# Cross-covariance attention and a GELU layer on one Trainium2 core: token blocks of 1024 in place of 512, other PSUM banks and a new order

## The chip, the core and the metric

The kernel runs on one core of a Trainium2 chip. Its engines run side by side, each with its own queue of instructions that it takes in order: TensorE (PE in the profile: matrix products, whose results go to PSUM), VectorE (DVE), ScalarE (ACT), GpSimd (POOL, used here mostly to issue DMAs), and SyncE (SP, issues DMAs). PSUM has 8 banks of 512 float32 per partition. The metric is the device time of one launch in microseconds.

## The reference

```python
qn = q / (norm(q, axis=1) + 1e-6)          # q, k, v: 4 x 6080 x 256, float32
kn = k / (norm(k, axis=1) + 1e-6)
a  = softmax(kn.T @ qn / tau, axis=-1)     # 256 x 256 per batch
x  = (v @ a).reshape(24320, 256)
h  = x @ w_in                              # 256 -> 2048
g  = 0.5*h*(1 + tanh(sqrt(2/pi)*(h + 0.044715*h**3)))
out = g @ w_out                            # 2048 -> 256
```

## The kernel before

**What it computes.** `v @ a @ w_in` is taken as `v @ (a @ w_in)`: per batch a matrix `AW` of 256 x 2048 is made from the scores, and then all 6080 tokens of the batch go through two products, `v . AW` (inner length 256, two halves `cc`) and `gelu(...) . w_out` (inner length 2048, in two halves `f` of 8 chunks of 128). All products take bfloat16.

**Scores of a batch.** q and k are loaded as bfloat16 in chunks of 6 rows per partition by `load_one` (L94, issued on the POOL queue; batch 0 has chunks of 8 and is loaded ahead of everything, L105 to L143). `square` (L181) squares a chunk on ScalarE or VectorE, `fold` and `fold_more` (L218, L226) add its rows on VectorE, `sum_parts` (L231) sums over partitions by a product. `gram_row` (L245) adds one row of `q.T k` to the running sum `G`, in bank `a`. A chain of small steps (L283 to L469) turns `G` and the norms into `AW`. For batches 1 to 3 this is spread between the token blocks of the batch before.

**Token blocks.** There are 12 blocks a batch, 48 in all, of 512 tokens (the last of a batch has 448). v goes to DRAM as bfloat16 by `cast_v` (L147, POOL queue) and comes back transposed by `load_vt` (L157, SP queue); the first three blocks are transposed on TensorE (L318). `mm1` and `gelu` (L511, L529) are the plain way: two chunks of 128 hidden columns in a pair of banks (`h` or `b`), four 512-column products, one gelu of 1024 values. The other way is a *set*: seven half-size products in place of eight (Winograd's form of Strassen's method; the halves are the tokens, the inner length, and two hidden chunk pairs `pa`, `pb`). `small` (L576) issues the products 1 to 7 of a set, each two of 256 columns, into a running sum `RB` (bank `s` or `p`) and the pair `QP` (`h` or `b`); `set_step` (L614) is what stands between them: `cq` and `y5` on ScalarE, `ap` and `ax` on VectorE, and the gelus `Gq`, `Gr`, `Gx`. A set costs ScalarE and VectorE more than the plain way and saves TensorE an eighth. `sums_w` and `sums_v` (L540, L552) make the operands. Blocks have two or three sets of four chunk pairs each (`sets_of`, L507).

The second product is taken by sevens too, on the block before: `sums_1` and `sums_2` (L693, L699) are differences of 2048 values a partition on VectorE, called T1 to T4; `product` (L716) issues M1 to M7, 8 products of 256 columns each, into the halves `r` and `p` of one bank `r`; `mm2_step` (L785) has its copies (`y5`, `cq` on ScalarE) and sums (`ap`, `ax` on VectorE); `turn` (L768) transposes a quarter of 256 values in VectorE, and `store` (L827) writes it out on the SP queue.

**The order.** Tile inserts the semaphores, but not the order: under `manual_schedule` each engine runs its instructions in the order in which the program calls them. The strings in `ORDER` (L998), one for each block, list all steps by short names: `g0` is a plain pair, `G0` its gelu, `w1m5` product 5 of set 1, `w1cq` its copy, `M5A` half of product M5, `row2` a Gram row, `lq`, `lk`, `lv`, `lt` the loads of q, k, v and the transposed v, `qsq` a square; a suffix counts blocks ahead or behind. A load of q, k or v carries a wait on the last product issued before it (`GATE`). So an instruction whose data are late holds up what stands behind it on its engine.

Of the kernel before, what the change touches and what calls it, by code (L numbers as in the profile page):

```python
# [17 lines left out]
def kernel(  # L19
# [14 lines left out]
    FC = D // 128  # L34
    assert isinstance(tau, (int, float)), "tau expected as a trace-time scalar"
    inv_tau = 1.0 / float(tau)

    R = N // 128
    REM = N - R * 128
    BLK = 512
    NB = (N + BLK - 1) // BLK
    PAIRS = FC // 2
    PE_BLOCKS = 2

    const = ctx.enter_context(tc.tile_pool(name="const", bufs=1))
    qkp = ctx.enter_context(tc.tile_pool(name="qkp", bufs=5))
    sqp = ctx.enter_context(tc.tile_pool(name="sqp", bufs=2))  # L50
    a1p = ctx.enter_context(tc.tile_pool(name="a1p", bufs=1))
    smx = ctx.enter_context(tc.tile_pool(name="smx", bufs=1))
    awp = ctx.enter_context(tc.tile_pool(name="awp", bufs=2))
    vts = ctx.enter_context(tc.tile_pool(name="vts", bufs=4))
    gp = ctx.enter_context(tc.tile_pool(name="gp", bufs=2))
    t1p = ctx.enter_context(tc.tile_pool(name="t1p", bufs=1))
    tsp = ctx.enter_context(tc.tile_pool(name="tsp", bufs=1))
    t4p = ctx.enter_context(tc.tile_pool(name="t4p", bufs=2))
    swp = ctx.enter_context(tc.tile_pool(name="swp", bufs=2))
    tvp = ctx.enter_context(tc.tile_pool(name="tvp", bufs=2))  # L60
    xp = ctx.enter_context(tc.tile_pool(name="xp", bufs=1))
    ywp = ctx.enter_context(tc.tile_pool(name="ywp", bufs=2))
    cp = ctx.enter_context(tc.tile_pool(name="cp", bufs=1))
    yout = ctx.enter_context(tc.tile_pool(name="yout", bufs=3))
    dram = ctx.enter_context(tc.tile_pool(name="dram", bufs=5, space=bass.MemoryType.DRAM))

    pM = ctx.enter_context(tc.tile_pool(name="pM", bufs=1, space=bass.MemoryType.PSUM))  # L70
    pH = ctx.enter_context(tc.tile_pool(name="pH", bufs=1, space=bass.MemoryType.PSUM))
# [16 lines left out]
    def after(inst, gate):  # L88

        if gate is not None:  # L90
            tc.add_manual_dep(inst.ins, gate.ins.name, mybir.DependencyInfo(
                mybir.DependencyClass.Sync, mybir.DependencyReason.DATA), reason="pace")

    def load_one(b, c, which, gate=None):  # L94
        r0, n = chunks_of(b)[c]
        t = qkp.tile([128, 8, 256], BF16, tag="qk"[which])
        src = (q, k)[which]
        after(nc.gpsimd.dma_start(  # L98
            out=t[:, 0:n, :],
            in_=src[b, 0 : R * 128, :].rearrange("(p r) c -> p r c", r=R)[:, r0 : r0 + n, :]), gate)  # L100
        if with_rest(b, c):
            after(nc.gpsimd.dma_start(out=t[:REM, n, :], in_=src[b, R * 128 : N, :]), gate)
        qk_tiles.setdefault((b, c), [None, None])[which] = t

    def load_first():  # L105


        r0, n = chunks_of(0)[0]
        assert not with_rest(0, 0)
        st = gp.tile([128, 2, n, 256], FP32, tag="g", name="qk_f32")  # L110
        for h in range(2):
            for which, eng in ((0, nc.sync), (1, nc.scalar)):
                eng.dma_start(out=st[:, which, h * 4 : h * 4 + 4], in_=(q, k)[which][0, 0 : R * 128, :].rearrange(
                    "(p r) c -> p r c", r=R)[:, r0 + h * 4 : r0 + h * 4 + 4, :])
        return st

    def cast_first(st):
        for which in range(2):
            t = qkp.tile([128, 8, 256], BF16, tag="qk"[which], name=f"first{which}")
# [7 lines left out]
    def load_qk(b, c):  # L127
        load_one(b, c, 0)
        load_one(b, c, 1)

    PIECES = [(0, 0, 4), (1, 0, 5), (1, 5, 8), (0, 4, 6), (0, 6, 8)]

    def load_last():
# [3 lines left out]
        qk_tiles[0, c] = [qkp.tile([128, 8, 256], BF16, tag="qk"[w], name=f"last{w}") for w in range(2)]  # L139
        for w, a, e in PIECES:  # L140
            nc.gpsimd.dma_start(
                out=qk_tiles[0, c][w][:, a:e, :],
                in_=(q, k)[w][0, 0 : R * 128, :].rearrange("(p r) c -> p r c", r=R)[:, r0 + a : r0 + e, :])  # L143

    v_bf = {}

    def cast_v(n, gate=None):  # L147
        b, blk = divmod(n, NB)
        t0 = blk * BLK
        cols = min(BLK, N - t0)  # L150
        vb = dram.tile([BLK, C], BF16, tag="vb", name=f"vb{n}")
        after(nc.gpsimd.dma_start(out=vb[:cols, :], in_=v[b, t0 : t0 + cols, :]), gate)
        v_bf[n] = vb

    vt_tiles = {}

    def load_vt(n):  # L157
        b, blk = divmod(n, NB)
        t0 = blk * BLK
        cols = min(BLK, N - t0)  # L160
        vT = vts.tile([128, 2, BLK], BF16, tag="vT")
        nc.sync.dma_start_transpose(out=vT[:, :, :cols], in_=v_bf.pop(n)[:cols, :])
        vt_tiles[n] = vT


    G, SS, SQ, SQR = {}, {}, {}, {}
# [8 lines left out]
    def new_squares(b, c):  # L175
        sq = sqp.tile([128, 8, 512], BF16, tag="sq", name=f"sq{b}_{c}")
        if with_rest(b, c):
            nc.vector.memset(sq[REM:, chunks_of(b)[c][1], :], 0.0)
        SQ[b, c] = sq

    def square(b, c, which, eng):  # L181
        if (b, c) not in SQ:
            new_squares(b, c)
        t = qk_tiles[b, c][which]
        n = chunks_of(b)[c][1]
        parts = [(128, slice(0, n))]
        if with_rest(b, c):
            parts.append((REM, slice(n, n + 1)))
        for np_, r in parts:
            o = SQ[b, c][:np_, r, which * 256 : which * 256 + 256]  # L190
            if eng == "act":
                nc.scalar.activation(o, t[:np_, r, :], AF.Square)  # L192
            else:
                nc.vector.tensor_mul(o, t[:np_, r, :], t[:np_, r, :])

    def square_rows(c, which, a, e, eng):
        if (0, c) not in SQ:
            new_squares(0, c)
        t = qk_tiles[0, c][which][:, a:e, :]
        o = SQ[0, c][:, a:e, which * 256 : which * 256 + 256]  # L200
# [5 lines left out]
    def fold_rows(b, c):  # L206

        n = len(rows_of(b, c))
        if n == 8:
            a1 = yout.tile([128, 4, 512], BF16, tag="ot", name=f"a1_{c}")  # L210
            nc.vector.tensor_add(a1, SQ[b, c][:, 0:4, :], SQ[b, c][:, 4:8, :])
            SQ[b, c] = a1
            n = 4
        SQR[b, c] = n

    FOLD = {}

    def fold(b, c):  # L218

        assert len(rows_of(b, c)) == 6  # L220
        sq = SQ.pop((b, c))
        a1 = a1p.tile([128, 3, 512], BF16, tag="a1", name=f"a1_{b}_{c}")
        nc.vector.tensor_add(a1, sq[:, 0:3, :], sq[:, 3:6, :])
        FOLD[b, c] = a1

    def fold_more(b, c, k):  # L226

        a1 = FOLD[b, c]
        nc.vector.tensor_add(a1[:, 0, :], a1[:, 0, :], a1[:, k - 1, :])

    def sum_parts(b, c):  # L231

        SS[b, c] = pM.tile([128, 4], FP32, tag="s", name=f"ss{b}_{c}")
        for j in range(4):
            nc.tensor.matmul(SS[b, c][:, j : j + 1], lhsT=FOLD[b, c][:, 0, j * 128 : j * 128 + 128],  # L235
                             rhs=ones_bf[:, 0:1], start=j == 0, stop=j == 3, skip_group_check=True)
# [8 lines left out]
    def gram_row(b, c, i):  # L245
        first = b not in G
        if first:
            G[b] = pM.tile([128, 2, 256], FP32, tag="a", name=f"G{b}")
        qt, kt = qk_tiles[b, c]
        rows = rows_of(b, c)  # L250
        r, np_ = rows[i]
# [8 lines left out]
    def ss_rows(c, which, rows=None):  # L260


        last = c == len(chunks_of(0)) - 1
        n = SQR.get((0, c), 8)
        rows = range(n) if rows is None else rows
        if c == 0:
            SS[which] = pM.tile([128, 2] if which == 0 else [128, 256], FP32,
                                tag="sp"[which], name=f"ss0{which}")
        sq = SQ[0, c]
        for r in rows:  # L270
            end = last and r == n - 1
            if which == 0:
                for jc in range(2):
                    nc.tensor.matmul(SS[0][:, jc : jc + 1],
                                     lhsT=sq[:, r, jc * 128 : jc * 128 + 128],
# [3 lines left out]
            else:  # L279
                nc.tensor.matmul(SS[1], lhsT=ones_bf, rhs=sq[:, r, 256:512],  # L280
                                 start=c == 0 and r == 0, stop=end)

    def g_copy(b):  # L283
        S = smx.tile([128, 2, 256], FP32, tag="S", name=f"S{b}")
        nc.scalar.activation(S, G[b], AF.Copy)
        G[b] = S

# [3 lines left out]

# [16 lines left out]
    V0 = []  # L308

    def load_v0(n):  # L310
        t = yout.tile([128, BLK // 128, C], BF16, tag="ot", name=f"v{n}")
        V0.append(t)
        nc.gpsimd.dma_start(out=t, in_=v[0, n * BLK : n * BLK + BLK, :].rearrange(
            "(s p) c -> p s c", p=128))

    VPS = {}

    def pe_vt(n, tag):  # L318

        VPS[n] = ps = pM.tile([128, 2, BLK], BF16, tag=tag, name=f"vt_ps{n}")  # L320
        for s in range(BLK // 128):
            for cc in range(2):
                nc.tensor.transpose(ps[:, cc, s * 128 : s * 128 + 128],
                                    V0[n][:, s, cc * 128 : cc * 128 + 128], ident_bf)

    def pe_vt_copy(n, cc):
        if n not in vt_tiles:
            vt_tiles[n] = vts.tile([128, 2, BLK], BF16, tag="vT", name=f"vT_pe{n}")
        nc.vector.tensor_copy(vt_tiles[n][:, cc, :], VPS[n][:, cc, :])

    def first_aw():

# [135 lines left out]

# [801 lines left out]
```

## Time and profile before

| | |
|---|---|
| median of 3 runs (lowest, highest) | 696.27 us (694.02, 703.08) |
| span of the profiled execution | 692.5 us |
| TensorE busy, matrix products | 671.3 us, 97%, 5643 records |
| VectorE busy | 630.7 us, 91%, 1111 |
| ScalarE busy | 624.0 us, 90%, 945 |
| DMA moved | 79.08 MB; mean busy share of the 16 DMA engines 0.9 and more in the first 100 us |
| granted TensorE clock | 0.999 |

The page gives the span of the profiled execution, from its first to its last instruction, and no time of the launch around it; the span lies 1.5 us under the fastest run and 3.8 us under the median. In the answers of the trace a row of a timeline is: start in us, duration in us, engine, line, operation, tiles, form, count, and in brackets the idle time before it with what ended it. The duration of a group of products reaches from the first start to the last end, and products overlap: the distance of starts is what the engine can sustain.

### The profile page before, as it was taken

To read this page: it belongs to the slowest core of one execution; us is meant where nothing else is said; L and a number is where in the kernel's file an instruction comes from. 1 tells how busy PE (TensorE), PEld (TensorE's weight loads), DVE (VectorE), ACT (ScalarE), POOL (GpSimd) and SP (SyncE) were. 2 spreads that over 40 slices of the span, in tenths; PEclk is the share of its full clock that TensorE was granted. 3 is DMA by queue.
4 is the path that set the end of the run, shared out by engine and by line. 5 is a ranking of instruction groups with operands and counts; after the bars stand their busy time and mean duration, and the time that the engine had idled before them with its cause. 6 is when DMAs were issued, how large, how long until landed. Compare 5 with 4: busy or idle time off the path is not lost.

```text
span 692.5 us, 14625 instructions
## 1 busy us (share of the span) xinstructions
PE 671.3 (97%) x5643; PEld 543.7 (79%) x5707; DVE 630.7 (91%) x1111; ACT 624.0 (90%) x945; POOL 74.4 (11%) x135
## 2 busy tenths in 40 slices
PE   3999999999999999999999999999999999999997
PEld 2856788888778888788877888878778888788886
DVE  3589999999999999999999999999999999899984
ACT  5379899999999899999999999999988999999984
POOL 4320111101001100110200011100100000000000
PEclk9999999999999999999999999999999999999999
DMA  9999799876766965686959495564263657142543
GB/s 242 207 269 130 138 153 132 119 126 107 129 117 111 164 94 92 100 144 110 140 83 156 85 162 89 98 103 85 33 107 60 104 93 100 39 77 47 94 71 59
DMA packets 161462, 79.08 MB, mean 114 GB/s; under 512 B 148448, under 2 KB 152160, under 8 KB 160672
## 3 DMA queue, kind: packets, MB, share of 16 engines
q0 software_dynamic: 14448, 39.72, 35.0%
q1 hardware_dynamic: 145696, 37.14, 32.4%
q10 hardware_dynamic: 1248, 1.28, 0.6%
q8 instruction: 44, 0.72, 0.5%
q14 instruction: 26, 0.21, 0.1%
HBM read 78.91 MB, written 36.57 MB: 167 GB/s over the span
## 4 chain that ended last, share of the span: by engine, by line
PE 88%; DMA 5%; issue 3%; ACT 2%; POOL 0%; DVE 0%; DVEq 0%; POOLq 0%
PE rp L736 39%; PE rb L604 15%; PE h L521 14%; PE qp L604 11%; PE G L253 5%; DMA t<-in_k_dram 4%; DMA t<-in_q_dram 1%; PE awp L454 1%; PE o L748 1%; ACT g L630 0%; ACT yw L623 0%; POOL t L98 0%; ACT qp L620 0%; ACT g L638 0%; PE ss L235 0%
## 5 line engine op out<-in xcount | busy, mean ns | idle before, releaser
L736 PEld LDWEIGHTS <-wcomb 128*128 128x128 bf16 x2632 | 255.4, 98 | 40.8 <-issue 1.6
L736 PE MATMUL rp<-t,wcomb 128*128 128x256 bf16 (+1 forms) x1504 | 208.1, 272 | 0.3
L736 PE MATMUL rp<-g,wcomb 128*128 128x256 bf16 (+1 forms) x1128 | 160.7, 272 | 0.1
L531 ACT ACTIVATE g<-h 128x1024 bf16<-128x1024 f32 (+1 forms) x136 | 137.5, 1017 | 12.5 <-PE h L521 10.9
L630 ACT ACTIVATE g<-qp 128x1024 bf16<-128x1024 f32 (+1 forms) x124 | 125.0, 1015 | 6.1 <-PE qp L604 3.9
L604 PEld LDWEIGHTS <-sw 128*128 128x128 bf16 x992 | 96.5, 98 | 22.9 <-issue 1.4
L521 PE MATMUL h<-vT,aw 128*128 128x512 bf16 (+1 forms) x406 | 111.8, 376 | 2.6
L625 DVE TENSOR_TENSOR qp<-rb,yw 128x512 f32<-128x512 f32 (+1 forms) x124 | 85.3, 689 | 9.4 <-PE rb L604 3.1
L604 PE MATMUL rb<-tv,sw 128*128 128x256 bf16 (+1 forms) x496 | 93.0, 271 | 0.1
L628 DVE TENSOR_TENSOR xw<-rb,yw 128x512 f32<-128x512 f32 (+1 forms) x124 | 83.7, 676 | 2.0 <-PE rb L604 1.0
L521 PEld LDWEIGHTS <-aw 128*128 128x128 bf16 x544 | 52.8, 98 | 38.9 <-DVE aw L362 0.6
L604 PEld LDWEIGHTS <-aw 128*128 128x128 bf16 x744 | 72.4, 98 | 12.9 <-issue 0.2
L638 ACT ACTIVATE g<-xw 128x512 bf16<-128x512 f32 (+1 forms) x124 | 77.3, 625 | 1.9 <-DVE xw L628 1.3
L620 ACT ACTIVATE qp<-rb 128x512 f32<-128x512 f32 (+1 forms) x124 | 72.3, 584 | 7.3 <-PE rb L604 3.2
L623 ACT ACTIVATE yw<-qp 128x512 f32<-128x512 f32 (+1 forms) x124 | 73.3, 596 | 3.0 <-PE qp L604 1.3
L635 ACT ACTIVATE g<-rb 128x512 bf16<-128x512 f32 (+1 forms) x124 | 72.5, 594 | 2.7 <-PE rb L604 2.2
L192 ACT ACTIVATE sq<-t 128x1536 bf16<-128x1536 bf16 (+4 forms) x49 | 64.5, 1336 | 6.1 <-DMA t<-in_q_dram 6.0
L774 DVE STREAM_TRANSPOSE ot<-rp 128x256 f32<-128x256 f32 (+1 forms) x141 | 59.8, 435 | 6.2 <-PE rp L736 4.8
L253 PE MATMUL G<-t 128*128 128x256 bf16 (+1 forms) x352 | 58.3, 276 | 1.3 <-DMA t<-in_k_dram 1.3
L711 DVE TENSOR_TENSOR t<-g,t 128x2048 bf16<-128x2048 bf16 (+1 forms) x47 | 56.7, 1206 | 0.7
L709 DVE TENSOR_TENSOR t<-g 128x2048 bf16<-128x2048 bf16 (+1 forms) x47 | 56.5, 1202 | 0.5 <-ACT g L638 0.4
L696 DVE TENSOR_TENSOR t<-g 128x2048 bf16<-128x2048 bf16 (+1 forms) x47 | 56.4, 1200 | 0.1
(131 smaller groups left out, 808.5 us busy)
## 6 DMA issues: line engine op xcount, KB each, us to landing
out_dram<-ot SPq DMA_DIRECT2D x174, 128.0 KB, 3.1
vb<-in_v_dram POOLq DMA_DIRECT2D x41, 256.0 KB, 4.9
t<-in_q_dram POOLq DMA_DIRECT2D x21, 384.0 KB, 5.7
t<-in_k_dram POOLq DMA_DIRECT2D x21, 384.0 KB, 4.9
wst<-in_moe_w_out_dram POOLq DMA_DIRECT2D x2, 1024.0 KB, 11.0
t<-in_q_dram POOLq DMA_DIRECT2D x3, 512.0 KB, 14.3
t<-in_k_dram POOLq DMA_DIRECT2D x3, 512.0 KB, 17.0
out_dram<-ot SPq DMA_DIRECT2D x12, 112.0 KB, 3.1
```

The lines of the kernel that those rows point to most:

```text
L253: nc.tensor.matmul(G[b][:, jc, :], lhsT=qt[:np_, r, jc * 128 : jc * 128 + 128], rhs=kt[:np_, r, :], start=first and jc == 0, stop=jc == 1, ...
L521: mm = nc.tensor.matmul(hp[:, u, :cols], lhsT=AW[b][:, cc, fc * 128 : fc * 128 + 128], rhs=vt_tiles[n][:, cc, :cols], start=cc == 0, stop= ...
L531: nc.scalar.activation(gs(n)[:, 2 * p : 2 * p + 2, :cols], HP.pop((n, p))[:, :, :cols], AF.Gelu_apprx_tanh)
L604: GATE[0] = nc.tensor.matmul(acc[:, u * hc : u * hc + hc], lhsT=lhs[:, u * 128 : u * 128 + 128], rhs=rhs, start=m in (1, 5) and u == 0, st ...
L620: nc.scalar.activation(qp(n, i)[:, 0, :c], RB[n, i][:, :c], AF.Copy)
L623: nc.scalar.activation(YW[n, i][:, :c], qp(n, i)[:, 1, :c], AF.Copy)
L625: nc.vector.tensor_add(qp(n, i)[:, 1, :c], RB[n, i][:, :c], YW[n, i][:, :c])
L628: nc.vector.tensor_add(XW[n, i][:, :c], RB[n, i][:, :c], YW.pop((n, i))[:, :c])
L630: nc.scalar.activation(gs(n)[:, 2 * pa : 2 * pa + 2, :c].rearrange("p u (t x) -> p t u x", t=2), QP.pop((n, i))[:, :, :c].rearrange("p t ( ...
L635: nc.scalar.activation(gs(n)[:, 2 * pb : 2 * pb + 2, :hc], two(RB.pop((n, i))[:, :c]), AF.Gelu_apprx_tanh)
L638: nc.scalar.activation(gs(n)[:, 2 * pb : 2 * pb + 2, hc:c], two(XW.pop((n, i))[:, :c]), AF.Gelu_apprx_tanh)
L736: nc.tensor.matmul(ACCS[n, acc][:, :hc], lhsT=wcomb[:, w, fc, :], rhs=x, start=first and k == 0, stop=k == 3, skip_group_check=True)
```

## The change

Every part of the kernel is written anew; the arithmetic is the same.

- **Blocks** are of 1024 tokens (the last of a batch 960; the last batch ends with 512 and 448): 25 blocks in place of 48. A plain step (`plain`) is one hidden chunk for 1024 tokens. Block 0 takes its tokens by halves (`half`, named `e` and `E`), all plain.
- **Sets** are of one chunk pair for 1024 tokens: a product of a set is one of 512 columns, not two of 256. A set is as much work as before. Six sets of eight in most blocks, three in block 1; over all there are 135 sets, of which 6 stand in the two small blocks, in place of 124.
- **Second product**: M1 to M7 have 512 columns. The sums `r` and `p` take a bank each, chosen in the order, in place of halves of one. T1 to T4 are as long as before, but T3 is written over a quarter of the gelu's result; there are two buffers each for T1/T4 and T2. `ap`, `ax`, `cq`, `y5` and the transposes work on 512 values, not 256.
- **Gram rows** come in three bursts a batch. A burst has its own running sum in whatever bank the order names; `gram_out` copies the first to SBUF on ScalarE and adds the next two there on VectorE.
- **Banks** `a`, `r`, `s`, `p` are named word by word in the order (`m1.1@r:1`), and no bank is kept for one purpose.
- **Buffers**: two of 1024 tokens for the transposed v, not four of 512; one for the v sums, not two; batch 0's q and k and `w_out` lie in the gelu buffers `g0b`, `g1a`, `g1b` ahead of their use, so that `w_out`'s first load waits for batch 0's last Gram row.
- **Order**: one string of words `step.args@bank:block`, new throughout. Ahead of it the loads are issued as before, but batch 0's v comes partly between those of `w_in`, and only tokens 0 to 1535 of v are transposed on TensorE, as before.

```diff
-    BLK = 512
+    for b in range(B):
+        sizes = [1024] * (N // 1024) + [N % 1024]
+        if b == B - 1:
+            sizes[-1:] = [512, N % 1024 - 512]
...
+    def gram_out(b):
+        g = G.pop(b)
+        if b not in GS:
+            GS[b] = smx.tile([128, 2, 256], FP32, tag="S", name=f"S{b}")
+            nc.scalar.activation(GS[b], g, AF.Copy)
+        else:
+            nc.vector.tensor_add(GS[b], g, GS[b])
...
-    def mm1(n, p):
+    def plain(n, u, tag):
+        b, _, t = BLOCKS[n]
+        hc = t // 2
+        hp = bank(tag, [128, 2, 512], f"h{n}_{u}")
...
+        for x in range(2):
+            BITS[tag, x] = w
+            for cc in range(2):
+                mm(hp[:, x, :w],
+                   lhsT=aw(b, cc, u if wide else 2 * u + x),
+                   rhs=vt_tiles[n][:, cc, x * hc : x * hc + hc] if wide else vt_tiles[n][:, cc, :],
+                   start=cc == 0, stop=cc == 1)
...
     def small(n, i, m, tag=None):
+        U = 1 if hc > 256 else 2
...
-        for u in range(2):
-            GATE[0] = nc.tensor.matmul(acc[:, u * hc : u * hc + hc], lhsT=lhs[:, u * 128 : u * 128 + 128],
-                             rhs=rhs, start=m in (1, 5) and u == 0, stop=u == 1,
-                             skip_group_check=True)
+        for u in range(U):
+            mm(acc[:, u * hc : u * hc + hc], lhsT=lhs(u), rhs=rhs,
+               start=m in (1, 5) and u == 0, stop=u == U - 1)
...
+    def token_sum(n, i, h):
+        if i == 3:
+            o = quarter(n, 0, 1, h)
+        else:
+            o = tp.tile([128, 4, 512], BF16, tag="tx" if i in (1, 4) else "ty", name=f"t{i}{h}_{n}")[:, :, :hc]
...
-    BANK = {1: "r", 2: "r", 3: "r", 5: "p", 6: "p", 7: "p", 4: "p"}
-                    rp = pM.tile([128, BLK], FP32, tag="r", name=f"rp{n}")
-                    ACCS[n, "r"], ACCS[n, "p"] = rp[:, 0 : BLK // 2], rp[:, BLK // 2 : BLK]
+        acc = "r" if i <= 3 else "p"
+        first = i in (1, 5) and (n, acc) not in ACC
+        if first:
+            ACC[n, acc] = bank(tag, [128, 512], f"{acc}{n}")
...
-    """g0 lv+3 aw3 G0 aw2 g1 ac2 ac3 aw4 G1 aw5 lq+1 ac4 g2 ac5 g3 G2 aw6 G3 g4 ac6 SW0 aw7 G4 g5
-    lk+1 ac7 vtp G5 pA11 g6 vtc0 g7 vtc1 G6 T1a vtq G7""",
+ORDER = """
+lq.0:1 e.1_0@h:0 lk.0:1 E.1_0:0 aw.2@s:0 aw.3@a:0 e.0_0@b:0 ac.2:0 vp.1@r:0 ac.3:0 e.3_0@h:0
+vc.1_1:0 vc.1_0:0 aw.5@p:0 aw.4@s:0 ac.5:0 lq.1:1 E.0_0:0 aw.6@a:0 E.3_0:0 qsq.0:1 e.2_0@b:0
+e.0_1@h:0 lv.1:1 E.2_0:0 E.0_1:0 aw.7@r:0 e.3_1@b:0 E.3_1:0 e.2_1@h:0 vp.0@p:1 e.1_1@b:0 E.2_1:0
+ac.4:0 ac.6:0 lk.1:1 SW.0:0 e.4_0@h:0 E.1_1:0 row.0_5@s:1 ksq.0:1 e.5_0@b:0 lv.0:2 pA11:0 E.4_0:0
...
```

## The prediction

> **What bounds the kernel now.** I read the page's totals first, then the busy time by stage, then single rows of the timelines.
>
> ```profile
> span 692.5 us, 14625 instructions
> ...
> PE 671.3 (97%) x5643; PEld 543.7 (79%) x5707; DVE 630.7 (91%) x1111; ACT 624.0 (90%) x945; POOL 74.4 (11%) x135
> ```
>
> ```profile
> 100.00:150.00 50.00, 49.74 (x434) 41.26 (x437) 47.27 (x83) 48.34 (x73) 6.91 (x13) 1.00 1.01 136
> 200.00:250.00 50.00, 49.74 (x432) 42.03 (x436) 47.70 (x90) 45.08 (x74) 5.25 (x11) 1.00 0.74 126
> 400.00:450.00 50.00, 49.82 (x436) 41.91 (x438) 46.73 (x81) 49.25 (x73) 5.69 (x11) 1.00 0.68 116
> ```
>
> The columns of the second are the stretch, its length, and the busy time of TensorE, its weight loads, VectorE and ScalarE. From 40 to 680 us TensorE is idle for some 4 us in all; it is the bound. But ScalarE and VectorE stand at 90 to 98% of the same stretches: there is little room under it. The first 37 us are another stage: batch 0's loads keep the DMA engines full and TensorE waits for data.
>
> Whether TensorE is busy says nothing of its pace. That is read from runs of equal products:
>
> ```profile
> start us, us, engine line op out<-in xcount [idle before <-releaser]
> 6.85 1.89 PE L253 MATMUL G<-first,first 128*128 128x256 bf16 x8 [6.85 <-ACT first L122]
> 28.60 1.91 PE L253 MATMUL G<-t 128*128 128x256 bf16 x16 [0.60 <-DMA t<-in_k_dram]
> 41.11 1.89 PE L521 MATMUL h<-vT_pe,aw 128*128 128x512 bf16 x8
> ```
>
> One product of 256 columns lasts 0.27 us, so 15 starts of the second row take 1.64 us: 109.4 ns each. Eight of 512 columns (41.11 to the next row at 42.84) take 1.73: 216.2 ns. The two fit 2.6 ns a product and 0.417 ns a column. The first row, after an idle start, has half that pace: 7 starts in 1.47 us, 210 ns for 256 columns.
>
> **The change part by part.**
>
> *Products.* From the two programs I count 5,704 products of 1,551,408 columns before and 3,576 of 1,545,648 after. The fewer columns are eleven more sets (135 for 124), each with an eighth less. 2,128 x 2.6 ns = 5.5 us, 5,760 x 0.417 ns = 2.4: **-7.9 us**, all on the path while TensorE is the bound. Width alone is nearly worthless, since time goes by columns. The Trainium skill (TensorE: Matmul & The Clock Gate, "Back-to-back issue gap") gives 131 ns as the sustained distance of 512-column products in a real stream and 216 ns as that of isolated ones; the trace's 216.2, taken in a stream with weight loads, is the second.
>
> *ScalarE and VectorE.* Eleven more sets cost ScalarE 0.588 + 0.600 + 0.598 + 0.630 + 1.024 us for two gelus of 1.025 each: +15 us of row means. Copies of the second product are half as many and twice as long, 0.59 for 2 x 0.37: -7.5. Squares moved to VectorE: -3. In sum ScalarE +4. VectorE: +15 for `ap`, `ax` of the added sets; v sums of 1024 values in fewer instructions -11; second product's sums (0.69 for 2 x 0.43) -7; transposes of 512 values, which the trace does not show: 0.44 at least, as for 256, 0.87 at most, as for two; I take 0.66, since the add grows by 1.6 from 256 to 512. That is -16 for 92 of them, with 20 either way. The six new adds of Gram sums are 0.69 each, as `ap`: +4. With the rest VectorE -7. None of this is on the path by itself.
>
> *Where they stand in the order.* I cut both orders into twelve stretches of 53.5 us of products and sum each engine's row means there (less 0.07 us an instruction on ScalarE, 0.055 on VectorE: their means add up to 693 us each, busy is 624 and 631, as neighbours overlap). Before, the worst stretch has 53.5 us of TensorE, 55.6 ScalarE, 56.6 VectorE; the trace shows no idle TensorE there, so about 3 us is carried by buffers. After, the fourth has 54.0, **59.3**, 55.9, and the seventh 53.6, 57.3, 56.6; the excess of all stretches is 11 us for 4 before. What passes 3 us of carry is 3.6 here and 2.7 to 6.5 with other cuts. I take **+5 us**; the bounds are 0 and the whole excess with shorter cuts, 15 above before's.
>
> *The first load of batch 1.* This is a wait that the change adds. The 21st word of the new order, `qsq.0:1`, puts the square of q's first chunk of batch 1 on ScalarE, ahead of the gelu `E.2_0`. In the old order the chunk is used 13 us of products after its load is issued. Here it is 5. When does it land? The rows of before:
>
> ```profile
> 36.23 0.90 POOL L655 DMA_DIRECT2D wst<-in_moe_w_out_dram  x1 [0.21 <-PE vt_ps L323]
> 38.98 0.54 POOL L152 DMA_DIRECT2D vb<-in_v_dram  x1 [1.86 <-PE h L521]
> 40.72 0.57 POOL L98 DMA_DIRECT2D t<-in_q_dram  x1 [1.19 <-PE h L521]
> ```
>
> ```profile
> wst<-in_moe_w_out_dram POOLq DMA_DIRECT2D x1, 1024.0 KB, 12.4
> t<-in_q_dram POOLq DMA_DIRECT2D x1, 384.0 KB, 10.8
> ```
>
> The second fence is the DMA view of those two issues, the last number being us from issue to landing. `w_out`'s second half lands at 48.6 us, v's cast at 49.7, q at 51.5, the k after it at 53.3: loads of the POOL queue land one by one in the order of issue, 1.8 us for 384 KB. After the change the same bytes stand ahead of that q but for v's cast. Issued at 37 instead of 41, it lands at **50.4**: earlier issue does not help, the bytes ahead do. ScalarE is at `qsq.0:1` at 42.6. TensorE's products up to `e.3_1` sum to 7.4 us from 37.65, so it reaches it at 45.0 and needs bank `b` there, which `E.2_0` frees: 50.4 + 1.4 (the square) + 1.0 = 52.8. **+7.8 us**. (VectorE waits likewise for k, until 52.2, with the copy `ac.7` behind it; TensorE wants that copy 8 us of products later: nothing more.) Below: if q were to land 4.9 us after issue, the median later on, nothing.
>
> *The pace after it.* The first bursts of the trace (idle to 6.85, then from 8.74 to 11.67) run at half pace until about 18.4, some 3.5 us of unbroken products. No row has a long idle time behind the full pace; the nearest is this start. So the loss is between nothing and half of 3.5 us; I take **+1.7**. The profile's granted clock, 1.00 there, does not show it. The Trainium skill (TensorE: Matmul & The Clock Gate, "Part 1: The HAM clock gate") has it as a rule, 1.2 GHz after an idle window of 3.4 us and 2.4 after a busy one; by it the loss is an estimated 1.7 us too. The trace agrees in so far as the two bursts, of 1.9 us each, did not bring the full pace and 3.5 unbroken us did.
>
> *Other waits.* Transposed v has two buffers, not four: counting from the store ahead of it on SP and the cast, the shortest leads of its 45 loads are 6.3, 6.9 and 9.7 us for 10.8 before, landing is 2.8 to 12.8, median 4.5. Loads of q and k have leads of 5.4, 5.6, 5.9 us where 8.1 was the shortest; they land in 4.2 to 11.9, median 4.9. The last block's stores have block 23's last quarter behind them, one more transpose and issue. Together **+1.5**, at most 6. Between a bank's last product and the next owner's first there are at least 0.43 us of products, as before (0.44), also with sums in banks of their own: nothing. `w_out`'s first load waits for batch 0's last Gram row (34.2 us, before it left at 33.6), behind a queue full until 40: nothing. The first 37 us are DMA's in both.
>
> *The sum*: -7.9 + 7.8 + 1.7 + 5 + 1.5 = +8.1. The span goes from 692.5 to 700.6. The span lies 3.8 us under the median of the runs, 696.27; with the same around it the time is **704 us**, 1.2% slower, which 2%, about what a measurement of this kernel can tell, calls no change.
>
> **The rivals.**
>
> *No wait and an order that fits* (0.24). Loads land in time, buffers carry the stretches: -7.9 + 2 gives 690. For it: before hides 3 us in a stretch. Against: loads landed in order without exception.
>
> *ScalarE and VectorE become the bound* (0.27). If the carry ends where a stretch is over by more than about 1 us, in place of 3, the excess of shorter cuts counts, 15 us for 5, and a longer transpose adds to it: 714 to 720, slower by over 2%. For it: after 37 us ScalarE and VectorE each need 96% of TensorE's time by these sums, for 94 and 96 before. Against: before shows next to none of it.
>
> *Wide products overlap in a long stream* (0.02), so that time no longer goes by columns and TensorE is not the bound. ScalarE is then: 624 + 4 us of work, and before's idle 21 up to 40 us and 8 after 680: 657, with 3.8 around it 661. The row with 216.2 ns speaks against it. The Trainium skill's 131 ns, named above, is this rival's rule.
>
> **How the numbers follow.** Forecast 0.47, its own range 698 to 710 by the stretches' and the other waits' ends. The range 690 to 718 leaves out the third rival, about half of the first (under 690), and the far end of the second. Faster by over 2% (under 682) 0.03: -7.9 alone ends at 688. Slower by over 2% (over 710): 0.27. Within: 0.70.
>
> **What would show it.** Right: groups of 512-column products at 216 ns; ScalarE's waits led by `sq` for `in_q_dram`, 7 to 8 us, ahead of the fourth gelu; TensorE idle from 45 to about 53 and the products after it at 430 ns for 512 columns; idle TensorE at 200 to 255 us, where the fourth stretch lies. Wrong: that q landing before 45; TensorE with under 6 us of idle time after 60; ScalarE's sum over 645.

## The result, and the profile after

The changed kernel takes **764.89 us** (median of 4 runs, 764.42 to 765.68) beside 695.16 us for the kernel before (694.02 to 703.08): a ratio of 1.098, 95% interval 1.092 to 1.104. It is 10% slower. The forecast was 704 with a range of 690 to 718, so it was wrong in size and in verdict.

The page's totals:

```profile
span 763.2 us, 10047 instructions
...
PE 687.0 (90%) x3518; PEld 336.5 (44%) x3579; DVE 629.6 (82%) x931; ACT 628.3 (82%) x935; POOL 74.4 (10%) x137
```

The work of VectorE and ScalarE is what it was (630.7 and 624.0 before), in a span that is 70.7 us longer. No engine is full. Busy time by stage (stretch, length, TensorE, weight loads, VectorE, ScalarE, POOL, granted clock, DMA share, GB/s):

```profile
40.00:60.00 20.00, 12.82 (x61) 6.08 (x60) 10.38 (x18) 9.34 (x10) 1.61 (x3) 0.83 0.83 205
100.00:150.00 50.00, 47.20 (x244) 22.96 (x248) 44.49 (x66) 46.22 (x67) 6.35 (x11) 1.00 0.67 105
200.00:250.00 50.00, 47.02 (x215) 20.83 (x218) 45.80 (x70) 42.95 (x67) 4.68 (x9) 1.00 0.60 99
400.00:450.00 50.00, 46.02 (x220) 20.59 (x223) 45.99 (x70) 45.87 (x68) 5.24 (x10) 1.00 0.79 129
```

One loss is early, as forecast. The other runs through the whole kernel: TensorE, which stood at 49.7 to 49.8 of 50 us, is at 46 to 47, and the two others fall with it. The waits (engine, tile and line, what it waited for: us in total, times, longest) say between whom:

```profile
PE qp L482 <- DVE qp L605: 13.9, 20, 1.2
...
PE rb L482 <- ACT qp L600: 8.0, 17, 0.7
PE e L482 <- ACT g L525: 7.0, 1, 7.0
PE qp L482 <- ACT yw L603: 5.6, 12, 1.3
...
ACT qp L600 <- PE qp L482: 32.2, 52, 1.7
...
DVE qp L605 <- ACT yw L603: 25.8, 33, 2.3
DVE qp L605 <- PE qp L482: 20.8, 22, 2.8
```

Of these rows all but the wait of `e` are steps of the sets, and most concern `qp`, the pair of banks that a set works in. Before, `cq` lost almost nothing to products that write the pair:

```profile
ACT qp L620 <- PE qp L604: 1.6, 3, 0.8
```

The chain of work that ended last shows the same, first for the changed kernel, then for the kernel before:

```profile
PE 63%; ACT 19%; DVE 9%; issue 3%; DMA 3%; POOL 0%; DVEq 0%; POOLq 0%; SPq 0%; ACTq 0%
```

```profile
PE 88%; DMA 5%; issue 3%; ACT 2%; POOL 0%; DVE 0%; DVEq 0%; POOLq 0%
```

What such a wait is can be seen in one set (timeline: start, duration, what, and the idle time before it with its releaser):

```profile
318.00 0.38 PE L482 MATMUL qp<-tv,sw 128*128 128x512 bf16 x1
...
318.41 0.58 ACT L600 ACTIVATE qp<-rb 128x512 f32<-128x512 f32 x1 [1.24 <-PE qp L482]
...
319.05 0.38 PE L482 MATMUL rb<-tv,sw 128*128 128x512 bf16 x1 [0.67 <-ACT qp L600]
...
319.38 0.60 ACT L603 ACTIVATE yw<-qp 128x512 f32<-128x512 f32 x1
...
320.04 0.38 PE L482 MATMUL qp<-vT,aw 128*128 128x512 bf16 x1 [0.62 <-ACT yw L603]
...
320.25 1.89 PE L482 MATMUL r<-g,wcomb 128*128 128x512 bf16 x8
...
320.45 0.70 DVE L605 TENSOR_TENSOR qp<-rb,yw 128x512 f32<-128x512 f32 x1 [1.51 <-PE qp L482]
```

These are product 5, `cq`, product 6, `y5`, product 2 and `ap` (and, at 320.25, eight products of the second product). Product 5 writes the second bank of the pair. `cq` copies `rb` into the *first* bank and reads nothing that product 5 makes; product 1, which it copies, had ended at 316.2. ScalarE stood idle for 1.24 us ahead of it, and it began 30 ns after product 5 ended. Product 2 adds to the first bank and waits for `y5`, which reads the second. `ap` writes the second bank and waits for product 2, which writes the first. These three waits have no datum behind them. The pair is one tile of 128 x 2 x 512, and the program's waits in PSUM are drawn by whole tile: the second bank is taken for the first. The wait of product 6 for `cq` is a true one (it adds to the bank that `cq` reads), and passes the delay on.

This was so before the change, too; the new order makes these pairs of steps neighbours more often. Counted in the two programs, before to after: `cq` waits for a product 5 issued behind product 1, from which `cq` has its data, in 40 of 124 sets, then in 89 of 135; product 2 stands ahead of `ap` in none, then in 45; after the change, product 2 waits for `y5` of its own set in 25.

**Where the 70.7 us are.** TensorE goes on to its next product 2.6 ns + 0.417 ns a column after the last one began, when nothing holds it (the forecast's term). What the distances of starts exceed that by is time without starts (times from the first counted instruction, 0.24 us into the span; products that the trace lacks are made up for):

| us | 0 to 40 | 40 to 60 | after 60 | start of the last product |
|---|---|---|---|---|
| before | 11.1 | 0.1 | 7.7 | 687.3 |
| after | 11.6 | 9.8 | 73.6 | 755.3 |

Without them the products take 668.4 and 660.3: **-8.1**. (This figure uses the forecast's own pace, so it does not test it. The row at 320.25 does: eight products of 512 columns in 1.89 us, as at 41.11 us before.) To that come +0.5 and +9.7 in the first two columns, **+65.9** in the third, and 2.7 more behind the last product's start: 70.7.

### The profile page after: what moved, and what is told of

It is laid out like the page before. It is cut to its first block, busy times and chain, and to the rows that moved or that the text cites. A ratio compares the mean times of both kernels' runs of the same rounds, so it can differ in the third digit from the quotient of the medians.

```text
span 763.2 us, 10047 instructions
## 1 busy us (share of the span) xinstructions
PE 687.0 (90%) x3518; PEld 336.5 (44%) x3579; DVE 629.6 (82%) x931; ACT 628.3 (82%) x935; POOL 74.4 (10%) x137
## 4 chain that ended last, share of the span: by engine, by line
PE 63%; ACT 19%; DVE 9%; issue 3%; DMA 3%; POOL 0%; DVEq 0%; POOLq 0%; SPq 0%; ACTq 0%
PE p L482 15%; PE rb L482 11%; PE r L482 11%; PE qp L482 9%; PE h L482 9%; ACT qp L600 5%; PE G L205 4%; ACT yw L603 4%; DVE qp L605 3%; ACT g L624 3%; ACT g L613 2%; ACT g L505 2%; ACT sq L158 2%; DVE t L691 2%; DMA q<-in_q_dram 2%
## 5 line engine op out<-in xcount | busy, mean ns | idle before, releaser
L482 PEld LDWEIGHTS <-wcomb 128*128 128x128 bf16 x1408 | 136.3, 97 | 166.9 <-issue 27.9
L482 PE MATMUL p<-t,wcomb 128*128 128x512 bf16 (+2 forms) x564 | 142.1, 372 | 1.3 <-ACT g L624 0.4
L605 DVE TENSOR_TENSOR qp<-rb,yw 128x512 f32<-128x512 f32 (+2 forms) x135 | 92.9, 689 | 60.1 <-ACT yw L603 25.8
L482 PE MATMUL r<-g,wcomb 128*128 128x512 bf16 (+2 forms) x564 | 140.8, 372 | 1.6 <-ACT p L751 0.9
L600 ACT ACTIVATE qp<-rb 128x512 f32<-128x512 f32 (+2 forms) x135 | 78.3, 583 | 42.6 <-PE qp L482 32.2
L691 DVE TENSOR_TENSOR t<-g,t 128x2048 bf16<-128x2048 bf16 (+2 forms) x96 | 113.0, 1183 | 0.1
L482 PE MATMUL rb<-tv,sw 128*128 128x512 bf16 (+3 forms) x281 | 98.7, 367 | 12.4 <-ACT qp L600 8.0
L505 ACT ACTIVATE g<-h 128x1024 bf16<-128x1024 f32 (+1 forms) x94 | 95.4, 1024 | 13.2 <-PE h L482 12.7
L608 DVE TENSOR_TENSOR xw<-rb,yw 128x512 f32<-128x512 f32 (+2 forms) x135 | 91.4, 678 | 15.3 <-PE rb L482 10.2
L482 PE MATMUL h<-vT,aw 128*128 128x512 bf16 (+2 forms) x383 | 98.6, 376 | 1.3 <-ACT g L613 0.2
L603 ACT ACTIVATE yw<-qp 128x512 f32<-128x512 f32 (+2 forms) x135 | 79.9, 595 | 8.4 <-PE qp L482 6.5
L482 PE MATMUL qp<-tv,sw 128*128 128x512 bf16 (+3 forms) x141 | 49.8, 367 | 4.1 <-ACT g L505 2.6
```

What stands on the lines that cost most here:

```text
L482: GATE[0] = nc.tensor.matmul(*a, skip_group_check=True, **kw)
L505: nc.scalar.activation(g_half(n, u // 8)[:, u % 8].rearrange("p (t x) -> p t x", t=2), hp[:, :, :hc], AF.Gelu_apprx_tanh)
L600: nc.scalar.activation(QP[n, i][:, 0, :w], RB[n, i][:, :w], AF.Copy)
L603: nc.scalar.activation(YW[n, i][:, :w], QP[n, i][:, 1, :w], AF.Copy)
L605: nc.vector.tensor_add(QP[n, i][:, 1, :w], RB[n, i][:, :w], YW[n, i][:, :w])
L608: nc.vector.tensor_add(XW[n, i][:, :w], RB[n, i][:, :w], YW.pop((n, i))[:, :w])
```

## The experiments

The texts on record name the explanations by letters. P is the waits between a pair's two banks. L is the load of the engines, ScalarE and VectorE having too much to do beside TensorE (the forecast's second rival). T is an order that leaves too little time between steps that truly depend on each other. B, in the text of the first reordered kernel, is the shared banks or the two buffers of v. The texts also work with a replay of the order, which is an estimate: each engine takes its instructions in the program's order, with durations from the trace and the traced delays between engines. It gives 689 us for before and 755 for after, where the spans are 692.5 and 763.2. It knows nothing of how loads share the DMA engines.

### The two banks as two tiles

```diff
-            QP[n, i] = bank(tag, [128, 2, 512], f"qp{n}_{i}")
+            QP[n, i] = pair(tag, f"qp{n}_{i}")
...
-            nc.scalar.activation(QP[n, i][:, 0, :w], RB[n, i][:, :w], AF.Copy)
+            nc.scalar.activation(QP[n, i][0][:, :w], RB[n, i][:, :w], AF.Copy)
...
-                nc.scalar.activation(g[:, k0].rearrange("p (t x) -> p t x", t=2), qp[:, :, :hc],
+                ge = nc.scalar.activation(g[:, k0].rearrange("p (t x) -> p t x", t=2), twice(qp[0], hc),
```

Every pair, those of the plain steps too, is two tiles of one bank. A gelu can read only one tile, so it reads the first bank twice. What this kernel leaves out is the gelu of the second banks; the number of values and the waits are the same. The order is the changed kernel's.

> The changed kernel in its own order, but the two banks of a pair (tags h and b) are two tiles, so that a step on one bank no longer waits for a step on the other. A gelu over a pair reads its first bank twice (as many values in the same form, so ScalarE's work is the same), and waits for the last products of both banks; what is left out is the gelu of the second banks. Theory P (pair): in the changed kernel 'cq' waits for m5 in 89 of 135 sets, m2 for 'ap' in 38, 'ap' for m2 in 26 and 'y5' for 'cq' in 94, and these waits, not the load, hold the engines. An estimate: each engine takes its instructions in this order, with the durations and hops of the trace (37 ns from a product's end to ScalarE or VectorE, 51 to 53 ns back); that gives 755 us for the changed kernel's span of 763, and 692 without the waits inside pairs. So P expects a span of 692 to 705, with under 20 us of idle TensorE after 60 us, for 74. Theory L (load; the rival B of the prediction): ScalarE and VectorE do as much work in the same order, so the span stays at 750 to 763. Theory T (the order leaves too little time between steps that truly depend on each other): most of the loss stays, over 740.

Measured: **702.51 us** in one execution, span 700.7. The page, the busy time of a stretch, and of TensorE's waits the longest and the longest for a step of a set:

```profile
PE 672.5 (96%) x3579; PEld 335.0 (48%) x3579; DVE 624.3 (89%) x931; ACT 616.8 (88%) x935; POOL 73.8 (11%) x137
```

```profile
400.00:450.00 50.00, 50.00 (x273) 24.90 (x271) 48.71 (x73) 49.21 (x75) 5.50 (x11) 1.00 0.73 125
```

```profile
PE e L491 <- ACT g L536: 7.1, 1, 7.1
...
PE qp L491 <- ACT qp L618: 0.4, 1, 0.4
```

TensorE is full again from 400 to 450 us; its waits for the steps of a set, 13.9, 8.0 and 5.6 us above, are down to 0.4 at most. Time without starts after 60 us falls from 73.6 to 11.3. So **62 us** of the loss are waits between two banks of one pair. L falls with it: ScalarE and VectorE do nearly the same work here (616.8 and 624.3 us for 628.3 and 629.6) and the span is 62.5 us shorter. So does T, which expected over 740: the steps that truly depend on each other stand as they did. Late loads after 60 us are out as well, since the loads are the same.

### Two of the waits put back

In the kernel with the banks apart, `cq` is made to wait for product 5 again; in another, product 2 and `ap` wait for each other again, in the changed order's direction. The gelu of the second banks is left out in both.

```diff
+            cq = nc.scalar.activation(QP[n, i][0][:, :w], RB[n, i][:, :w], AF.Copy)
+            after(cq, M5[n, i])
```

```diff
+            if m == 2 and u == 0:
+                after(GATE[0], AP.get((n, i)))
...
+            after(AP[n, i], M2.get((n, i)))
```

> As e1_halves_apart (702.5 us; it leaves out the gelu of the second banks), and one of the waits put back by hand: each 'cq' waits for m5 of its set, which writes the other bank of the pair. Theory P with this wait as the main part: by the order with the trace's durations 692 becomes 725, so 702 becomes 730 to 738, and ScalarE's waits are led by 'cq' for m5. If the waits matter only together (theory P, all at once): under 715.

> As e1_halves_apart (702.5 us; the gelu of the second banks is left out), and the other wait put back: of m2 and 'ap' of a set, which write the two banks of the pair, the one that is issued later waits for the one issued earlier (45 sets have m2 first, 90 'ap'). By the order with the trace's durations 692 becomes 716, so 702 becomes 722 to 730. If 'cq' alone is the cause: 702 to 707.

Measured, in one execution each: 734.43 us and 725.94 us, so +31.9 and +23.4 for two kinds of wait that no datum needs. The waits of the first:

```profile
ACT qp L620 <- PE qp L491: 33.0, 56, 1.7
```

and of the second, `ap` for product 2 and TensorE for `ap`:

```profile
DVE qp L627 <- PE qp L491: 12.1, 13, 1.9
...
PE qp L491 <- DVE qp L627: 12.5, 19, 1.1
```

The same rows stand in the changed kernel, with 32.2, 20.8 and 13.9 us. After 60 us the time without starts is 43.7 and 34.9 for 11.3: +32.4 and +23.6, together 56 of the 62. The rest, `y5` behind `cq` and the plain pairs, was not tried by itself.

### The same wait in the kernel before

If this is the cause, the kernel before must lose time by it as soon as its order is made like the new one. Its word for product 2 is moved directly behind product 6, ahead of `ap`, in 114 of the 124 sets; nothing else is changed.

```diff
...
-    lk+1 T3-1 lq+1 w0m6 w0ap M4B-2 M4A-2 c21-2 row0 c12-2 w0m7 w0m2 w0ax g0 qsq-1 w0m3 w0m4 G0
...
+    w0m5 T4-2 w0cq w0y5 lt+2 g5 G5 row1-1 ax-2 lk+1 T3-1 lq+1 w0m6 w0m2
+    w0ap M4B-2 M4A-2 c21-2 row0 c12-2 w0m7 w0ax g0 qsq-1 w0m3 w0m4 G0 T1a-1
...
```

> The kernel before with one product moved: in 114 of its 124 sets m2 stands directly behind m6, ahead of 'ap' on the same pair, and not behind 'ap'. Nothing that m2 needs is late there (it adds to what 'cq' copied). Theory P: 'ap' now waits for m2 and m3 for both; by the order with the durations of the trace before, 689 becomes 714, so the time goes from 695 to 715 to 725. Theory L: no work is added and no engine has more in a stretch, 693 to 698. Theory T: m2 does not depend on 'ap' and stands further from m3, so nothing is lost, 693 to 698.

Measured: 718.31 us, ratio 1.034 (1.032 to 1.036). The waits of VectorE are led by

```profile
DVE qp L625 <- PE qp L604: 14.3, 36, 1.0
DVE qp L625 <- ACT yw L623: 9.7, 12, 1.3
```

`ap` waits for product 2, which writes the other bank, 36 times. Neither L nor T, which both expected 693 to 698, had this. Narrow products and 512-token blocks suffer from such an order as wide ones do; width is not the cause.

### The first square moved back

```diff
-vc.1_1:0 vc.1_0:0 aw.5@p:0 aw.4@s:0 ac.5:0 lq.1:1 E.0_0:0 aw.6@a:0 E.3_0:0 qsq.0:1 e.2_0@b:0
+vc.1_1:0 vc.1_0:0 aw.5@p:0 aw.4@s:0 ac.5:0 lq.1:1 E.0_0:0 aw.6@a:0 E.3_0:0 e.2_0@b:0 e.0_1@h:0
...
+lk.1:1 SW.0:0 e.4_0@h:0 E.1_1:0 row.0_5@s:1 ksq.0:1 e.5_0@b:0 lv.0:2 pA11:0 E.4_0:0 qsq.0:1
```

> The changed kernel with one word moved: qsq.0:1, the square of batch 1's first chunk of q, stands behind the gelu E.4_0 and no longer ahead of E.2_0. The prediction's step on it: 7.8 us of idle TensorE and 1.7 of slow products go, 765 becomes 755. By the order taken with the trace's durations only 3 us are left of it at the end, as the sets behind it wait for each other anyway: 762. Theories P, L and T say nothing else of it.

The early loss as the changed kernel has it (timeline):

```profile
50.22 1.48 ACT L158 ACTIVATE sq<-q 128x1536 bf16<-128x1536 bf16 x1 [6.97 <-DMA q<-in_q_dram]
...
52.67 1.86 PE L482 MATMUL e<-vT,aw 128*128 128x512 bf16 x4 [7.02 <-ACT g L525]
```

Measured with the square later: 760.4 us, ratio 1.095 (1.092 to 1.097), **4.5** less than the changed kernel, not the 9.7 that the stretch holds. TensorE goes past the square and stops at the next thing that needs the same row of loads:

```profile
52.32 0.38 PE L205 MATMUL G<-k,q 128*128 128x256 bf16 x2 [2.65 <-DMA k<-in_k_dram]
```

The time without starts there goes from 9.8 to 5.2.

### The changed kernel in other orders

The same steps, banks and buffers as in the changed kernel, but the words of its order string in another sequence, searched by the replay. Only `ORDER` differs; here its first line of words in the last of the four:

```diff
-lq.0:1 e.1_0@h:0 lk.0:1 E.1_0:0 aw.2@s:0 aw.3@a:0 e.0_0@b:0 ac.2:0 vp.1@r:0 ac.3:0 e.3_0@h:0
+aw.2@s:0 ac.2:0 e.1_0@h:0 E.1_0:0 lv.1:1 lt.1:1 aw.3@a:0 e.0_0@b:0 E.0_0:0 ac.3:0 lq.0:1 e.3_0@h:0
```

> The changed kernel with the same words, the same banks and the same turns of every buffer and bank, but in another order: words were moved, by up to some tens of places at a time, wherever the order with the trace's durations and hops (waits inside pairs among them) said that TensorE would wait less. By that it takes 685 where the changed kernel takes 755 to 760. Theories P and T, which both blame the order: 690 to 698, TensorE idle after 60 us for 10 to 16 us. Theory L: the engines' work is the same and near what they can do, so 720 or more. A theory that the shared banks or the two buffers of v are the cause (theory B): they are as they were, so 740 or more.

> As e4_words_reordered: the words, banks and turns of the changed kernel in another order. In e4, which took 718.7, TensorE waited 13.8 us for the transposed v and 4.4 for a chunk of k, with a slow clock behind: the order had been chosen with 4.5 us for every load. Here it was chosen with 9 us for the transposed v, and with loads of the POOL queue that land one behind the other, 2.0 us for 384 KB and 1.3 for 256. By that the products end 4 to 5 us before those of the kernel before. Theory P: 688 to 695, no change that 2% can tell from the kernel before, and as much as the prediction gave for an order that fits (690). If pair waits and loads are not all that the order lost: over 700.

> As e7: the words, banks and turns of the changed kernel in another order. In e7 (707.7 us) TensorE waited 12.4 us at 59 us for the first transposed v, which landed only with the last of a row of loads on the POOL queue; nothing else stood out. Here the order was chosen with 12.5 us for every transposed load and, as in e4 and e7, with such a load landing no earlier than 3.2 us after the POOL loads issued up to then. Taken with these times, the changed kernel's own order gives 765 (measured 764.9), e7's 708 (707.7), and this one 687. Theory P, with the loads as the only rest: 686 to 692, faster than the kernel before (694.6) by 0.4 to 1.2%. If the order loses by something else that e7's wait covered: 695 or more.

> As e9, found from another start: 687 by the same sum, so 686 to 692 again. If e9's time hangs on luck with single loads, the two differ by more than 5 us.

| order | us | ratio (95%) | longest wait for a transposed v, us |
|---|---|---|---|
| first | 718.70 | 1.036 (1.031 to 1.041) | 9.8 |
| second | 707.69 | 1.018 (1.015 to 1.021) | 12.4 |
| third | 713.09 | 1.026 (1.023 to 1.029) | 17.1 |
| fourth | 692.98 | 0.998 (0.997 to 0.999) | none |

The third's time is the median of five executions, 708.88 to 714.46; a sixth took 721.35. Three of the four passed the upper end of what was expected by 13 to 21 us, the fourth by 1. What the three share is a wait for a transposed v. TensorE's in the second order (timeline), and the busy time around it:

```profile
71.81 1.01 PE L482 MATMUL h<-vT,aw 128*128 128x512 bf16 x2 [12.41 <-DMA vT<-vb]
```

```profile
60.00:80.00 20.00, 8.19 (x32) 3.70 (x32) 5.13 (x8) 5.64 (x7) 0.00 (x0) 0.66 0.66 125
```

and in the third (its trace is of the execution of 721.35 us, so the others may have waited less), with the busy time just after it:

```profile
105.04 0.61 PE L482 MATMUL rb<-vT,aw 128*128 128x512 bf16 x1 [17.13 <-DMA vT<-vb]
```

```profile
108.00:112.00 4.00, 1.76 (x5) 0.64 (x5) 2.62 (x5) 3.59 (x4) 0.00 (x0) 0.50 0.07 15
```

A transposed load issued in the first 75 us, beside a full POOL queue, landed after 24.2 us in the first order, 21.9 in the second, 20.9 and 32.3 in the third; others in the four orders took 3.5 to 12.2 us, and in the changed kernel, with that queue empty, one took 3.2. The replay had them at 12.5 us at most. So single loads decide by 20 us which order is good: the last two orders look the same to the replay, and after 150 us their time without starts is the same, about 11 us each.

The fourth met no such wait: its page and a stretch of it.

```profile
PE 670.5 (97%) x3579; PEld 336.2 (49%) x3579; DVE 627.7 (91%) x931; ACT 624.3 (90%) x935; POOL 75.9 (11%) x137
```

```profile
100.00:150.00 50.00, 50.00 (x276) 25.39 (x275) 47.69 (x73) 48.09 (x72) 5.77 (x10) 1.00 0.68 104
```

692.98 us is 71.9 under the changed kernel and 0.2% under the kernel before, which by the 2% that count here is no change. Its waits between the banks of a pair are still drawn (product 2 stands ahead of `ap` in 25 sets, for 45), but TensorE has only 12.8 us without starts after 60 and 0.9 from 40 to 60. So wide blocks, other banks, bursts and six sets, taken together, cost nothing against the kernel before, which also rules B out; **the new order did, by where it put the steps of a set**.

### Narrow products

The second order, with every product of more than 256 columns issued as two halves: 6,223 products for 3,576.

```diff
+        c = w // 2 if w > 256 else w
+        for x in range(0, w, c):
+            GATE[0] = nc.tensor.matmul(out[:, x : x + c], lhsT=lhsT, rhs=rhs[:, x : x + c],
```

> As e7_words_reordered_again, with every product of more than 256 columns issued as two of half the columns into the same bank: 6,223 products for 3,576, the columns the same. The prediction's step on products (2.6 ns a product): 2,647 x 2.6 = 6.9 us more than e7, at most 1 us of it hidden in waits. If width were worth nothing: the same as e7. If wide products overlapped (the prediction's third rival, 131 ns for 512 columns): over 100 us more.

Measured: 712.41 us (711.37 to 712.61), 4.7 more than the second order's 707.69 (707.47 to 708.23). 2,647 starts of 2.6 ns are 6.9; 2.6 us less of time without starts after 60 us (12.9 for 15.5) make up for part of them. Width is worth a few us, as forecast, and time goes by columns.

## Why the prediction was wrong

**What held.** *Products*: -7.9 forecast, -8.1 measured at the forecast's pace, and that pace is the same in both kernels. *The first load of batch 1 and the pace after it*: +7.8 + 1.7 = 9.5, measured 9.7; q landed at 50.2 for 50.4, TensorE stood from 45.6 to 52.67, and the weight loads behind it stand 0.43 us apart, half pace. The two parts are off in opposite ways: 7.2 without starts for 7.8, and some 2.5 of slow products for 1.7. *ScalarE*: 628.3 for 624 + 4. *The transposes*: 0.70 to 0.71 us a piece where 0.66 was taken between 0.44 and 0.87; this is most of why VectorE has 629.6 us for the forecast's 630.7 - 7. *Stretches and other waits*: 6.5 in the sum; the kernel with the banks apart shows 3.6 after 60 us and 3.4 behind the last product's start, 7.0.

Its span is 700.7, the forecast 700.6: the forecast is that of a kernel in which the two banks of a pair are apart. That it fits to 0.1 us is luck. The stretches had +5 and *other waits* +1.5; measured are 3.6 and 3.4, and in the 50 us where the fourth stretch lies TensorE is idle for only 0.5 us. The 3.8 us added for what lies around the span was too much as well: it is 1.8 for the changed kernel (765.01 us for a span of 763.2), and the 3.8 came from a median of three runs with 703.08 among them.

**The step that failed** is the one headed ScalarE and VectorE, with its close "None of this is on the path by itself". It counted how much `cq`, `y5` and `ap` work, and the next one how that work stands to TensorE's in stretches of 53.5 us; neither asked, inside a set, which step is issued behind which and what it waits for. *Other waits* listed loads, stores and the hand-over of a bank to its next owner ("at least 0.43 us of products ... nothing"), but not the hand-overs inside the pair while one set owns it. That term was taken as nothing and measured 62 us. Everything for it was at hand: the old order had no set with product 2 ahead of `ap`, the new has 45, and the program lists the wait. The new order was costed only by the place of its loads and the sum of its work. The signs that the forecast named show this. ScalarE's wait at `sq` came as described (7.0 us) but did not lead its waits; `cq` for products on the pair did (32.2 us). Idle TensorE was not gathered at 200 to 255 us either; it is 2.8 to 4.0 us in each of the stretches of 50 us shown above.

**The rivals.** The first, an order that fits at 690, is what the fourth order is (692.98); the changed order is not it. The second, work of ScalarE and VectorE as the bound, has the right engines on the path for the wrong reason: it priced their durations, and with the same durations the span is 700.7 where the banks are apart. The third is out by the narrow products and by the row at 320.25: 216 ns from start to start of 512-column products in the changed kernel.

**Why the range failed.** Its upper end was built from the ends of the costed terms. A step that isn't costed has no end.

The Trainium skill (PSUM — Partial Sum Buffer, "Summary: rules for kernel authors") says to aim a read at a different bank from the one TensorE works on and to guard by bank. The runs show what a wider guard costs here: with the waits drawn by bank and not by tile of two banks, TensorE lost 62 us less. That the values stay right without the wider guard they do not show, as that kernel leaves out the gelu of the second banks.

## What to carry to other kernels

Before an order is costed by its sums, list for one repeated unit (here a set) every instruction's waits as the program has them, and look for those without a datum behind them; a tile that spans two PSUM banks makes its steps wait for each other across the banks. Either give each bank its own tile, or keep another unit's products between two such steps. And an order found by an estimate of waits is worth no more than that estimate's landing times: the four orders of one kernel lie 26 us apart, and waits for single loads are most of it.

## What the runs showed of the hardware

**Transposed loads beside a full POOL queue.** The view of the DMA queues (packets, MB, share of the span of 16 engines), for the changed kernel from 55 to 70 us and for the third order from 80 to 103 us:

```profile
q0 software_dynamic: 320, 1.05, 44.6%
q1 hardware_dynamic: 1305, 0.33, 9.7%
```

```profile
q0 software_dynamic: 544, 1.50, 63.5%
q1 hardware_dynamic: 1342, 0.33, 53.5%
```

`q1` carries the transposed loads. The same 0.33 MB in about 1,300 packets: one packet took 0.097 x 15 us x 16 / 1305 = 17.8 ns in the first and 147 ns in the second, 8 times as much. (The shares of the two queues add up to 117% in the second, so such a time holds waiting too.) Both sides were slow: a load of k issued on POOL at 74.8 us in the third order landed at 104.1. The Trainium skill (DMA: Bandwidth & Descriptors, "Queues, rings and completion order") has each engine take turns between queues by packet. If its packets are those that this view counts, POOL's are some eleven times as large as these (1.50 MB in 544), and a turn behind them is long, which fits the direction. No run here changes the POOL queue alone, so this is argued and not shown. Why the third order had 147 ns where the first, with POOL's queue fuller (86.9%), had 46 from 56 to 75 us, is open.

**The clock after a long wait.** The forecast found no granted clock under 1.00 at the slow start of before; the trace has no record of the clock there before 18.5 us, so that 1.00 is not a measurement. Behind idle times of 7 us and more a lower clock does show: 0.83 from 40 to 60 us in the changed kernel, 0.66 in the second order, 0.50 in the third, where the first product after 17.1 us of waiting took 0.61 us for 0.38. In the changed kernel it is 0.50 from 50.8 to 57.5 us and 1.00 in the 5 us before, so it fell some 5 us into the wait and came back some 5 us after the products did.
